# Another order of issue, and other engines for some steps, in a pooled-attention and gated-MLP kernel

## Chip, core and metric

The kernel runs on one core of one Trainium2 chip. The metric is device time in microseconds (us): the median over runs of the whole program. A core has five engines with queues of their own: TensorE (PE, matmuls; PEld are its weight loads), VectorE (DVE), ScalarE (ACT), GpSimd (POOL) and SyncE (SP), which here issues nearly all transfers.

## What is computed

Eight batches of attention with pooled keys and values, then a gated MLP whose gate mixes tokens:

```python
# pool = 8, B, H, S, D = 8, 8, 576, 64
k_p = k.reshape(B, H, S // 8, 8, D).mean(axis=3)
v_p = v.reshape(B, H, S // 8, 8, D).mean(axis=3)
attn = softmax(q @ k_p.T / sqrt(D))              # over the 72 pooled keys
x = (attn @ v_p)                                 # heads side by side: 576 x 512
u, v = split(gelu_tanh(x @ w_in), 2)             # 576 x 512 each
v_n = (v - mean) / sqrt(var + 1e-6) * g_ln
v_s = einsum('ts,bsd->btd', w_sg, v_n) + b_sg[None, :, None]
out = x + (u * v_s) @ w_out
```

All in 32-bit precision; `w_in` and `w_out` arrive as 64-bit floats and are cut into a high and a low 32-bit part on the chip. Every large product is the sum of three matmuls (high by high, high by low, low by high).

## The kernel before, in words

One core does the eight batches one after the other. The work of a batch is cut into steps, each a generator that issues some instructions and then yields. A hand-kept list, `ORDER`, names at each place which step goes on by one piece: `S1+3` is the next piece of step S for pair of heads 1 in batch 3. The lower-case names are the preparation of weights, once for the kernel. As every engine takes its queue in order, `ORDER` sets what each engine does after what. The last lines of the kernel tie each instruction to the one before it on its engine.

The steps of a batch, in the order of the data:

- A, B, C, E load keys, values, one pair's queries (a tile qT, four of them in turn) and the left-over values (through `load`, L234, on SyncE's queue). K sums the keys by eight (`sum8`, L355 on VectorE as one reduction, L358 and L359 on GpSimd as three additions) and lays them out for two heads (kbd); P does the same for values. In batch 0 both are matmuls.
- S (four, one for each pair of heads): scores (TensorE, into PSUM), the maximum (L486, VectorE), the softmax and a copy of a part (el, L503, GpSimd). T and L turn the result over, from batch 1 on through VectorE's 32x32 transpose and HBM. V multiplies by the values, and copies and splits the result into a high and a low part (xhl), with a small tile xta beside it.
- J (batch 0) and H (five blocks of tokens): the v half of the first projection, gelu, mean and variance, scaling, and the split into vhh and vhl. U (four): the u half. W (four): the token mixing into PSUM; then L695 and L697 on VectorE gate it with u, and ghi and glo are split from that. O (four): the second projection, and the sum with x. Z stores.
- Weights: v0 to v3 and u0 to u3 prepare w_in, o0 to o3 w_out, s0 to s4 w_sg. A piece of v, u or o is: one scaling on ScalarE (L275), three integer operations on VectorE (L277, L278, L279), a rounding on ScalarE (L283), then three operations called low, topd and lo below (L222 or L224, L231, L231). lv0, lv1, lu0, lu1, lo0, lo1 load a megabyte each, ls0 and ls1 the w_sg.

The second list, `OTHER`, is a set of keys. A helper that finds its key in it puts its operation on the other of two engines:

| helper | key in `OTHER` | key not in it |
|---|---|---|
| copy (L209, L211) | VectorE | ScalarE |
| move (L215, L217) | GpSimd | ScalarE |
| lower and lowest (low) | VectorE, one operation (L222) | ScalarE (L228) and GpSimd (L224) |
| combine (L231: topd, lo, the low parts) | VectorE | GpSimd |
| sum8 | VectorE, one reduction | GpSimd, three additions |
| normal (L443) | GpSimd | VectorE |
| soften, expo, total | VectorE adds and sums (L448, L462), one exponential (L453) | ten exponentials on ScalarE (L457) |
| scaled | VectorE (L467) | a short one on VectorE (L470), ScalarE (L471) |

A digit for the batch in a key is capped: m3x, k3x, V3x and the like stand for batches 3 to 7, G2x, W2x, H2x and g2x for batches 2 to 7. Exponential and gelu need different tables on ScalarE: where the two follow each other in its queue, `ready` (L204) puts a table load between them.

TensorE's order in batch 0 is: keys and scores, pooled values, T, L and V, then J, H4, U0 to U3 and W0 to W3, with the scores of batch 1 in between. From then on the S, T, L, V of the next batches run between H, U, W and O of the one before.

Of the kernel before, what the change touches and what calls it, by code (L numbers as in the profile page):

```python
# [37 lines left out]
W3+0 W3+0 V0+1 W2+0 A0+3 S2+2 L0+1 K0+3 W3+0 T1+1 T3+1 V0+1 S0+2 S0+2 O0+0 V0+1 T1+1 V0+1 T1+1 S2+2 S2+2 O0+0 V1+1
V1+1 T2+1 O0+0 O1+0 T2+1 S3+2 T0+2 T2+1 O1+0 V2+1 S2+2 P1+2 S1+2 E0+2 O2+0 T3+1 O2+0 O1+0 S3+2 S1+2 S1+2 T3+1 T3+1
V2+1 O3+0 O3+0 Z1+0 O2+0 K0+3 V1+1 O3+0 V3+1 V3+1 V3+1 V2+1 H0+1 H1+1 T0+2 S3+2 S2+2 H0+1 T0+2 V2+1 S3+2 C0+3 T1+2  # L40
V3+1 A1+3 C2+3 S0+3 S3+2 H0+1 L0+2 V1+1 H1+1 H1+1 P2+2 B0+3 H2+1 P2+2 P2+2 H0+1 L0+2 H2+1 H0+1 T0+2 S0+3 P2+2 H3+1
H4+1 H0+1 H3+1 L0+2 H1+1 H1+1 P2+2 H1+1 K1+3 L0+2 K1+3 S1+3 U0+1 Z0+0 V0+2 H3+1 H4+1 H4+1 U1+1 U0+1 C1+4 H2+1 B1+3
H3+1 H4+1 H2+1 T3+2 U1+1 L0+2 T1+2 Z3+0 Z2+0 U2+1 H3+1 U3+1 P0+3 H4+1 H4+1 T2+2 S1+3 T1+2 T1+2 V1+2 H2+1 U2+1 P1+3
U3+1 H2+1 A0+4 H3+1 V0+2 H4+1 H4+1 A1+4 W0+1 T2+2 S0+3 K1+4 W1+1 W0+1 T2+2 K0+4 V0+2 T2+2 E0+3 V1+2 V2+2 W1+1 W0+1
S2+3 V2+2 V1+2 V2+2 S2+3 C3+3 S0+3 T3+2 T3+2 T3+2 W2+1 K0+4 V3+2 S0+3 S1+3 T0+3 T0+3 S3+3 S1+3 V3+2 W3+1 W2+1 V3+2
H0+2 W3+1 V3+2 W1+1 W3+1 W2+1 V0+2 S2+3 S2+3 W0+1 W1+1 W3+1 S1+3 W2+1 P2+3 P2+3 P2+3 H0+2 H1+2 H1+2 H2+2 H0+2 C0+4
H2+2 C2+4 V2+2 T0+3 B0+4 S3+3 S0+4 H1+2 T1+3 T2+3 S0+4 S2+3 S3+3 P2+3 O0+1 O0+1 S3+3 S3+3 O1+1 H0+2 O0+1 Z0+1 O1+1
O1+1 P2+3 T0+3 H1+2 O2+1 H0+2 O2+1 V1+2 S1+4 L0+3 H2+2 L0+3 H1+2 H0+2 O2+1 H1+2 H3+2 S0+4 H3+2 H4+2 S0+4 S0+4 S1+4
H3+2 O3+1 O3+1 H4+2 L0+3 L0+3 H4+2 V0+3 H4+2 L0+3 H4+2 H4+2 P0+4 O3+1 U0+2 U1+2 T1+3 C1+5 Z1+1 Z2+1 T1+3 U0+2 U1+2
T0+4 T1+3 V1+3 T2+3 U2+2 U2+2 U3+2 Z3+1 T2+3 V1+3 H3+2 H3+2 H2+2 T2+3 B1+4 C3+4 H2+2 H2+2 V0+3 V0+3 V1+3 V1+3 K1+4  # L50
H4+2 H3+2 T3+3 H4+2 W0+2 S2+4 U3+2 W0+2 V2+3 S2+4 S1+4 W1+2 S2+4 S2+4 V2+3 A0+5 S3+4 S3+4 E0+4 S3+4 W1+2 W2+2 W2+2
K0+5 W2+2 W3+2 P1+4 T3+3 T3+3 T3+3 V3+3 W3+2 W0+2 W0+2 V2+3 W2+2 V3+3 T0+4 W3+2 W3+2 V3+3 H0+3 W1+2 A1+5 W1+2 S1+4
S1+4 H0+3 H0+3 T1+4 S3+4 S3+4 B0+5 C0+5 H1+3 H1+3 C2+5 O0+2 O0+2 O0+2 Z0+2 H0+3 V0+3 H0+3 H0+3 S2+4 T2+4 O1+2 O1+2
O1+2 V3+3 L0+4 L0+4 O2+2 O2+2 O2+2 O3+2 O3+2 V2+3 H1+3 P2+4 P2+4 P2+4 Z2+2 T0+4 K0+5 H1+3 H1+3 H1+3 O3+2 L0+4 Z1+2
S0+5 S0+5 H2+3 H2+3 T0+4 H3+3 K1+5 L0+4 L0+4 S1+5 H4+3 H3+3 P2+4 P2+4 C3+5 H3+3 H4+3 V0+4 H4+3 H3+3 E0+5 S0+5 P2+5
Z3+2 H4+3 U0+3 U0+3 H4+3 U1+3 S1+5 U1+3 C1+6 U2+3 H4+3 U3+3 S0+5 H4+3 T1+4 T1+4 U2+3 K1+5 V0+4 H2+3 H2+3 T1+4 V1+4
V1+4 U3+3 H4+3 H2+3 P0+5 H3+3 S0+5 T2+4 T3+4 C3+6 T2+4 H3+3 T2+4 A0+6 H2+3 W0+3 S2+5 S1+5 W0+3 W0+3 W0+3 V2+4 W1+3
W2+3 S2+5 V2+4 V2+4 S1+5 W1+3 T3+4 T3+4 T3+4 V3+4 B1+5 P1+5 A1+6 W1+3 V0+4 W1+3 W2+3 T0+5 C0+6 T0+5 P2+5 T1+5 W3+3
V1+4 W3+3 V3+4 V3+4 W3+3 V0+4 P2+5 S3+5 K0+6 S2+5 H0+4 H0+4 S2+5 H1+4 H2+4 S3+5 B0+6 H0+4 H1+4 W2+3 W2+3 V1+4 O0+3
W3+3 T2+5 H2+4 S3+5 O0+3 K0+6 H1+4 H1+4 H0+4 O0+3 S3+5 H2+4 H0+4 H2+4 T0+5 O1+3 O1+3 O2+3 O1+3 V3+4 Z1+3 P0+6 S0+6  # L60
O2+3 Z0+3 T0+5 S1+5 O3+3 V2+4 H0+4 O3+3 S0+6 P2+5 C2+6 S2+5 H1+4 O2+3 Z2+3 H1+4 O3+3 S3+5 P2+5 L0+5 H2+4 L0+5 S1+6
H3+4 H4+4 H3+4 K1+6 H4+4 H4+4 S1+6 U0+4 U0+4 U1+4 H4+4 H4+4 L0+5 L0+5 V0+5 U1+4 L0+5 U2+4 U3+4 S0+6 T1+5 T3+5 U2+4
C1+7 Z3+3 B1+6 H3+4 H3+4 T1+5 T1+5 V1+5 H4+4 H4+4 H3+4 H4+4 H3+4 T2+5 H2+4 W0+4 W0+4 S0+6 U3+4 W1+4 V0+5 K1+6 V1+5
T2+5 T2+5 P1+6 W1+4 A0+7 W1+4 W1+4 S1+6 E0+6 P2+6 S0+6 K0+7 V2+5 V2+5 V2+5 S2+6 S2+6 W2+4 W3+4 V2+5 T3+5 B0+7 W2+4
T3+5 T3+5 V3+5 V3+5 V1+5 W3+4 W3+4 V0+5 A1+7 S3+6 V3+5 K0+7 V1+5 W2+4 H0+5 H1+5 S2+6 W0+4 V3+5 S1+6 W3+4 T0+6 H0+5
W0+4 W2+4 S3+6 O0+4 H1+5 K1+7 S3+6 P2+6 K1+7 O0+4 P2+6 C0+7 T1+6 O1+4 O0+4 S0+7 C2+7 O1+4 T0+6 H1+5 H0+5 B1+7 O1+4
Z1+4 H0+5 S3+6 S3+6 S2+6 Z0+4 H1+5 H1+5 H2+5 H3+5 H2+5 T2+6 V0+5 O2+4 O2+4 S2+6 O2+4 Z2+4 H0+5 H0+5 H1+5 H3+5 S1+7
# [768 lines left out]
```

## Time and profile before

| | |
|---|---|
| median of 3 runs | 581.48 us (579.4 to 582.49) |
| the profiled execution | 582.18 us |
| its span, first to last instruction | 580.5 us |
| TensorE busy, mean granted clock | 538.5 us, 0.977 |
| VectorE, ScalarE, GpSimd busy | 429.4, 270.2, 280.3 us |

The span is 1.7 us short of the time of the same execution. The page gives the share of each engine, then the same in 40 slices of 14.5 us; the view by windows gives it for stretches of one's own choice, with the clock that TensorE was granted (1.00 is the higher of its two levels). A matmul counts as busy from start to modelled end, so TensorE's busy share says where it waits, not how fast it could be.

### The profile page before, as it was taken

The numbers are of one execution on the slowest core, as the hardware profiler recorded it, in microseconds if no ns is written. First come the engines' busy times: TensorE is split into PE (matmuls) and PEld (weight loads), VectorE is DVE, ScalarE is ACT, GpSimd is POOL, SyncE is SP. The second block draws the span as 40 slices with busy tenths as digits, with TensorE's granted clock in tenths as the row PEclk, the third lists the DMA queues.
The fourth block names the chain that finished last, engine by engine and source line by source line (L and its number), as shares of the span: only waits on it lengthen the run. The fifth ranks groups of instructions, "written<-read, shape, count | busy, mean of one in ns | idle before, by whom it ended". The sixth has DMA issues, their size and how long they took to land.

```text
span 580.5 us, 9490 instructions
## 1 busy us (share of the span) xinstructions
PE 538.5 (93%) x3552; PEld 502.9 (87%) x3552; DVE 429.4 (74%) x639; ACT 270.2 (47%) x533; POOL 280.3 (48%) x350
## 2 busy tenths in 40 slices
...
DVE  1799999898877898477978977678796876454252
...
GB/s 289 350 255 177 98 64 29 132 132 116 159 168 164 118 66 118 162 51 133 166 74 160 159 71 73 190 98 130 135 87 42 62 93 93 42 21 42 0 1 103
DMA packets 43134, 67.08 MB, mean 116 GB/s; under 512 B 5776, under 2 KB 22160, under 8 KB 43088
## 3 DMA queue, kind: packets, MB, share of 16 engines
...
q8 instruction: 28, 0.46, 0.3%
...
q14 instruction: 18, 0.15, 0.1%
...
## 4 chain that ended last, share of the span: by engine, by line
PE 59%; DVE 26%; DMA 4%; POOL 4%; issue 3%; ACT 2%; SPq 1%; DVEq 0%; POOLq 0%; ACTq 0%
PE mps L133 50%; PE aps L133 9%; DVE nmax L486 2%; DVE top L278 2%; DVE e L448 1%; SPq L234 1%; DVE ssum L462 1%; DVE bst L644 1%; DVE xhl L231 1%; DVE raw L279 1%; DVE al L561 1%; DVE top L231 1%; DMA al<-tfar 1%; DVE y L509 1%; DMA kraw<-in_k 1%
## 5 line engine op out<-in xcount | busy, mean ns | idle before, releaser
L133 PE MATMUL mps<-xhl,wih 128*128 128x288 f32 x512 | 90.2, 298 | 6.2 <-ACT vg L640 4.9
L133 PE MATMUL mps<-wih,xhl 128*128 128x512 f32 x256 | 84.4, 400 | 3.7 <-DVE xhl L231 2.4
L133 PEld LDWEIGHTS mps<-xhl,wih 128*128 128x128 f32 x512 | 75.9, 190 | 7.7 <-ACT vg L640 5.4
L443 POOL TENSOR_TENSOR e<-e,ssum 128x720 f32<-128x720 f32 x24 | 35.9, 1499 | 61.6 <-DVE ssum L442 61.6
L133 PEld LDWEIGHTS mps<-wih,xhl 128*128 128x128 f32 x256 | 47.7, 188 | 16.1 <-DVE xhl L231 3.9
L133 PE MATMUL mps<-wsh,vhh 128*128 128x288 f32 x256 | 56.5, 303 | 1.6 <-ACT u L681 1.6
L133 PE MATMUL mps<-wsh,vhl 128*128 128x288 f32 x256 | 55.9, 300 | 1.7 <-DVE vhl L231 1.7
L133 PE MATMUL mps<-wsl,vhh 128*128 128x288 f32 x256 | 56.0, 301 | 0.0
L133 PE MATMUL mps<-xhl,wil 128*128 128x288 f32 x256 | 54.8, 295 | 0.0
L133 PE MATMUL mps<-ghi,woh 128*128 128x288 f32 x240 | 51.6, 295 | 2.0 <-DVE x L733 2.0
L647 POOL TENSOR_TENSOR rstd<-mv,eps 128x1 f32<-128x1 f32 (+1 forms) x40 | 10.2, 255 | 86.1 <-DVE mv L645 84.4
L133 PE MATMUL mps<-glo,woh 128*128 128x288 f32 x240 | 51.4, 295 | 0.3 <-POOL glo L231 0.2
L133 PE MATMUL mps<-ghi,wol 128*128 128x288 f32 x240 | 51.3, 295 | 0.0
L133 PE MATMUL mps<-wil,xhl 128*128 128x512 f32 x128 | 50.5, 395 | 0.0
L231 POOL TENSOR_TENSOR xhl<-x,xhl 128x576 fp32r<-128x576 f32 x23 | 32.9, 1435 | 34.2 <-ACT x L211 30.6
L695 DVE SCALAR_TENSOR_TENSOR mps<-mps,gcol,bbc 128x576 f32<-128x576 f32 x32 | 26.3, 821 | 29.9 <-PE mps L133 29.7
L231 POOL TENSOR_TENSOR glo<-u,ghi 128x576 fp32r<-128x576 f32 x17 | 25.4, 1506 | 42.2 <-ACT ghi L211 38.3
L133 PE MATMUL aps<-kbd,qT 128*128 128x144 f32 x300 | 43.4, 293 | 1.9 <-ACT x L211 1.7
L133 PEld LDWEIGHTS mps<-wsh,vhh 128*128 128x128 f32 x256 | 42.4, 195 | 1.9 <-ACT u L681 1.8
L133 PEld LDWEIGHTS mps<-wsh,vhl 128*128 128x128 f32 x256 | 42.3, 194 | 2.0 <-DVE vhl L231 2.0
L133 PEld LDWEIGHTS aps<-kbd,qT 128*128 128x128 f32 x300 | 40.3, 194 | 3.6 <-ACT x L211 2.4
L644 DVE BATCH_NORM_STATS2 bst<-vg 128x6 f32<-128x512 f32 (+1 forms) x40 | 27.2, 680 | 20.9 <-ACT vg L637 11.6
...
## 6 DMA issues: line engine op xcount, KB each, us to landing
...
```

The costliest lines, as they stand in the source:

```text
L133: nc.tensor.matmul(o, lhsT, rhs, start=start, stop=stop)
L231: (nc.vector if key in OTHER else nc.gpsimd).tensor_tensor(o, x, y, op=op)
L234: queue.dma_start(o, i)
L278: nc.vector.scalar_tensor_tensor(top, high, -0x80000000, top, op0=ALU.bitwise_and, op1=ALU.bitwise_or)
L279: nc.vector.tensor_scalar(high, top, -0x800000, None, op0=ALU.bitwise_and)
L443: (nc.gpsimd if key in OTHER else nc.vector).tensor_tensor(e, e, rec.unsqueeze(3).broadcast_to([P, NT, 2, SP]), op=ALU.mult)
L448: nc.vector.tensor_tensor(e, every.rearrange("p s (h k) -> p s h k", h=2), nmax.unsqueeze(3).broadcast_to([P, NT, 2, SP]), op=ALU.add)
L462: nc.vector.tensor_reduce(out=ssum, in_=e, axis=AX.X, op=ALU.add)
L486: nc.vector.tensor_reduce(out=nmax, in_=every.rearrange("p s (h k) -> p s h k", h=2), axis=AX.X, op=ALU.max, negate=True)
L644: nc.vector.bn_stats(bst, vg)
L647: nc.gpsimd.tensor_tensor(rstd, mv[:, 1:2], eps[:n, 1:2], op=ALU.add)
L695: nc.vector.scalar_tensor_tensor(vs, vs, gcol[:, d:d + 1], bbc.rearrange("p (a n) -> p a n", a=2), op0=ALU.mult, op1=ALU.add)
```

## The change

Both lists are replaced. `ORDER` has the same 1252 entries, each as often as before, in another order. `OTHER` had 104 keys and has 117: 57 come in and 44 go out. No helper and no step is altered. The start of `ORDER` and the whole of `OTHER`:

```diff
 ORDER = """
-A0+0 C0+0 E0+0 lv0 v1 v1 A1+0 K0+0 K0+0 S0+0 H0+0 H1+0 v1 C1+0 S1+0 B0+0 S0+0 K1+0 v1 S0+0 B1+0 A0+1 C2+0 S1+0 S1+0
-S0+0 v0 C3+0 lv1 K0+1 v0 S1+0 K1+0 K0+1 S0+0 S1+0 T0+0 A1+1 S2+0 S2+0 v0 v3 v0 T0+0 P0+0 ls0 S2+0 S2+0 L0+0 s2 s3
-P1+0 s0 P0+0 lu0 B0+1 C0+1 L0+0 lo0 P1+0 V0+0 v3 v2 T1+0 E0+1 v2 s1 V0+0 V0+0 K1+1 S2+0 v3 s0 s1 v2 S3+0 S3+0 J0+0
-v2 s3 T1+0 V1+0 s2 v3 S3+0 u0 P0+1 u1 S3+0 u1 T2+0 V1+0 T2+0 u1 V1+0 S3+0 L1+0 T3+0 L1+0 u1 B1+1 V2+0 T3+0 u0 lu1 u3
-P1+1 u3 V2+0 u0 C1+1 u0 A0+2 V0+0 V3+0 S0+1 S0+1 u3 V3+0 u2 K0+2 C3+1 V2+0 u2 K1+1 u3 S0+1 S0+1 V2+0 J1+0 J2+0 V3+0
-J3+0 o1 o1 u2 u2 H1+0 H2+0 H1+0 C2+1 S1+1 S2+1 H0+0 H0+0 A1+2 K1+2 o1 P2+1 V1+0 P2+1 V3+0 H3+0 S1+1 H3+0 o0 H1+0 o0
-H1+0 o0 ls1 S0+1 H1+0 H2+0 S1+1 C0+2 o1 H4+0 U0+0 S3+1 H0+0 H0+0 H2+0 H0+0 H4+0 S2+1 o0 lo1 S2+1 H4+0 H3+0 U1+0 C1+2
-U0+0 C3+2 B0+2 o3 K0+2 H4+0 S1+1 U1+0 U2+0 B1+2 U3+0 S2+1 S1+1 o2 o3 S2+1 H2+0 H2+0 H4+0 o2 o2 s4 o3 H3+0 o2 P2+1
-T0+1 H2+0 H3+0 H3+0 H4+0 S3+1 C2+2 T0+1 H4+0 o3 H4+0 S0+2 U2+0 U3+0 T1+1 S3+1 s4 S0+2 W0+0 S3+1 S3+1 W0+0 L0+1 P2+1
...
+lv0 A0+0 v0 v0 E0+0 A1+0 C0+0 v1 v1 v1 v1 v0 K0+0 lv1 B0+0 K0+0 A0+1 v3 v0 v2 S0+0 S0+0 K1+0 v3 v2 C1+0 S0+0 K1+0 v3
+S0+0 C2+0 B1+0 K0+1 S1+0 S1+0 lu0 S2+0 S2+0 v2 K0+1 S1+0 S1+0 S0+0 S2+0 T0+0 v2 P0+0 v3 P0+0 S1+0 L0+0 S2+0 T0+0
+L0+0 P1+0 P1+0 V0+0 A1+1 ls0 s1 u0 u1 K1+1 s0 B0+1 C3+0 C1+1 lo0 V0+0 T1+0 T1+0 u0 u0 u1 s2 S3+0 S3+0 K1+1 S3+0 C2+1
+V0+0 V1+0 s2 B1+1 V1+0 lu1 J0+0 s1 ls1 u0 s0 C3+1 S2+0 u1 S3+0 S3+0 u2 T2+0 T2+0 P0+1 L1+0 L1+0 T3+0 V2+0 C0+1 T3+0
+u2 u2 s3 V1+0 u1 V2+0 u2 u3 A0+2 o0 H0+0 H1+0 H2+0 u3 V2+0 s4 o0 J1+0 u3 V3+0 V3+0 J2+0 V3+0 J3+0 u3 o0 s4 H0+0 H0+0
+V1+0 S0+1 o0 P1+1 H1+0 V3+0 S1+1 V2+0 E0+1 H2+0 o1 A1+2 V0+0 S0+1 S0+1 H0+0 H0+0 S1+1 H3+0 H1+0 H4+0 S2+1 S1+1 S0+1
+H0+0 H2+0 H3+0 S2+1 H1+0 o1 S3+1 lo1 H1+0 H1+0 o1 o1 o2 H4+0 H4+0 s3 C0+2 P2+1 P2+1 U0+0 U0+0 H4+0 K0+2 S2+1 H4+0
+H3+0 o3 U1+0 U2+0 U1+0 U2+0 P2+1 o2 H3+0 S0+1 o2 H3+0 H2+0 H4+0 H2+0 o3 o2 U3+0 U3+0 S2+1 T0+1 H2+0 S3+1 S2+1 C1+2
+T0+1 H4+0 o3 H3+0 S3+1 o3 H4+0 S1+1 S1+1 W0+0 W0+0 K1+2 K1+2 S3+1 W0+0 S3+1 B0+2 C3+2 T1+1 P0+2 L0+1 W1+0 P2+1 C2+2
...
 """.split()

 OTHER = set("""
-G00 G01 G12 G13 H00 H01 H03 H13 H21 H23 V00 V01 V11 V13 V33 W02 W03 W10 W20 W21 X10 X11 X20 X21 X30 X31 X32 c10 c12
-c22 g00 g04 g10 g13 g14 g21 g22 g23 g24 h11 h20 k10 k31 l2 l3 m00 m02 m10 m12 m21 m22 m23 m30 m31 m32 m33 n00 n01
-n11 n12 n13 n20 n21 n22 n23 n30 n31 n32 o0d o1m o2a o2d o2m o3a s0d s2 s2d s3 u0a u0d u0m u1a u1d u1m v0d v2a v2d
-v2m v3a x11 x13 x20 x21 x23 z00 z04 z11 z14 z22 z23 z31 z32 z33 z34
+G10 G12 G20 G21 G23 H00 H01 H03 H10 H11 H20 H23 V00 V02 V03 V12 V13 V21 V23 V30 V33 W01 W02 W11 W12 W13 W20 W21 W22
+W23 X10 X11 X12 X13 X20 X22 X23 X30 X31 X32 X33 c11 c22 g11 g14 g20 g22 g23 g24 h20 h21 k10 k11 k20 k21 l1 l2 l3 m01
+m11 m21 m22 m23 m30 m31 m32 m33 n00 n02 n10 n11 n20 n21 n22 n23 n30 n31 n32 o1d o1m o2d o2m p10 p11 s0d s1 s1d s2d
+s4d u0m u1a u1d u1m u2a u2d u2m u3d u3m v0a v0d v0m v1a v1d v1m v2a v2m v3a z00 z03 z11 z12 z14 z20 z24 z30 z32 z34
 """.split())
```

Told by the table above, the keys do this before the first gating of batch 0 (`W0+0`): on VectorE come in two key sums, two value sums and a left-over sum, four low, one topd, two splits of w_sg and one of xhl; from it go two soften and two total, two copies to vhh and one to w_sg. Ten-fold exponentials are then issued for six S steps instead of four. Counted through the list, the exponential and the gelu change places 35 times on ScalarE instead of 29.

## Rows read from the trace of the kernel before

**Rows 1.** The page, parts 1 and 2: busy time, share and count; tenths in 40 slices.

```profile
PE 538.5 (93%) x3552; PEld 502.9 (87%) x3552; DVE 429.4 (74%) x639; ACT 270.2 (47%) x533; POOL 280.3 (48%) x350
...
DVE  1799999898877898477978977678796876454252
```

**Rows 2.** The view by windows: stretch, length, each engine's busy time, clock, DMA share, GB/s.

```profile
0.00:14.50 14.50, 7.42 (x31) 7.29 (x32) 1.76 (x4) 3.89 (x7) 7.78 (x28) 1.00 0.86 290
14.50:106.78 92.28, 69.74 (x373) 58.06 (x372) 87.60 (x120) 62.42 (x170) 65.28 (x65) 0.91 0.49 163
107.00:215.00 108.00, 103.18 (x676) 96.43 (x676) 91.33 (x138) 49.25 (x101) 62.05 (x75) 0.97 0.46 130
215.00:560.00 345.00, 342.61 (x2364) 325.85 (x2363) 242.55 (x371) 153.07 (x254) 142.32 (x181) 1.00 0.32 94
```

**Rows 3.** Timeline of VectorE (start, length, group): first score maximum, first gating of batch 0.

```profile
14.57 0.91 DVE L486 TENSOR_REDUCE nmax<-mps 128x10 f32<-128x720 f32 x1 [1.87 <-PE mps L133]
...
106.78 0.80 DVE L695 SCALAR_TENSOR_TENSOR mps<-mps,gcol,bbc 128x576 f32<-128x576 f32 x1
```

**Rows 4.** Groups by form, VectorE, 14.5 to 106.8: busy, mean ns | idle before.

```profile
L278 DVE SCALAR_TENSOR_TENSOR top<-raw,top 128x512 int32<-128x512 int32 x11 | 11.8, 1077 | 0.4
L279 DVE TENSOR_SCALAR raw<-top 128x512 int32<-128x512 int32 x11 | 9.7, 882 | 0.4
...
L222 DVE SCALAR_TENSOR_TENSOR raw<-raw 128x512 f32<-128x512 uint32 x5 | 5.2, 1044 | 0.0
L231 DVE TENSOR_TENSOR top<-top,wih 128x512 f32<-128x512 f32 x4 | 5.2, 1300 | 0.0
L231 DVE TENSOR_TENSOR wil<-raw,top 128x512 fp32r<-128x512 f32 x4 | 4.2, 1043 | 0.1
L462 DVE TENSOR_REDUCE ssum<-e 128x10 f32<-128x720 f32 x4 | 3.5, 887 | 0.3 <-ACT e L453 0.3
L231 DVE TENSOR_TENSOR top<-top,woh 128x512 f32<-128x512 f32 x2 | 3.4, 1684 | 0.0
...
L231 DVE TENSOR_TENSOR wol<-raw,top 128x512 fp32r<-128x512 f32 x2 | 2.5, 1248 | 0.0
...
L355 DVE TENSOR_REDUCE kp<-kraw 128x144 f32<-128x1152 f32 x1 | 1.3, 1294 | 0.0
```

**Rows 5.** Weight tiles `top` and `raw`, VectorE: ns min/median/max, first and last start.

```profile
L278 DVE SCALAR_TENSOR_TENSOR top<-raw,top x12: 691/693/1787, 11.6 to 91.9; 128x512 int32<-128x512 int32 x12
...
L231 DVE TENSOR_TENSOR top<-top,wih x4: 679/1314/1892, 26.0 to 57.7; 128x512 f32<-128x512 f32 x4
...
L279 DVE TENSOR_SCALAR raw<-top x12: 427/428/1940, 12.3 to 92.7; 128x512 int32<-128x512 int32 x12
...
L222 DVE SCALAR_TENSOR_TENSOR raw<-raw x5: 686/949/1466, 40.2 to 94.6; 128x512 f32<-128x512 uint32 x5
```

**Rows 6.** Groups by form, GpSimd, the same stretch as in rows 4.

```profile
L224 POOL TENSOR_TENSOR raw<-raw 128x512 f32<-128x512 f32 x6 | 6.8, 1125 | 3.0 <-DVE raw L279 1.6 <-issue 1.1 <-ACT raw L228 0.2
...
L443 POOL TENSOR_TENSOR e<-e,ssum 128x720 f32<-128x720 f32 x4 | 5.9, 1488 | 5.2 <-DVE ssum L442 5.2
```

**Rows 7.** Timelines of TensorE, SyncE's queue and ScalarE: first matmul, weight load, weight step.

```profile
6.29 1.86 PE L133 MATMUL mps<-pool,kraw 128*128 128x16 f32 x8 [6.29 <-DMA kraw<-in_k]
...
1.83 0.57 SPq L234 DMA_DIRECT2D raw<-in_moe_w_in  x1
...
10.40 0.66 ACT L275 ACTIVATE top<-raw 128x512 f32<-128x512 f32 x1 [7.66 <-DMA raw<-in_moe_w_in]
```

**Rows 8.** ScalarE: table loads (groups); timeline: one wide exponential, first and last of ten.

```profile
L204 ACT ACT_TABLE_LOAD x29 | 37.2, 1283 | 0.5
...
16.46 0.80 ACT L453 ACTIVATE e<-e 128x720 f32<-128x720 f32 x1 [3.56 <-DVE e L448]
...
40.29 0.32 ACT L457 ACTIVATE e<-aps,nmax 128x72 f32<-128x72 f32 x1 [4.01 <-DVE nmax L486]
...
42.96 0.37 ACT L457 ACTIVATE e<-aps,nmax 128x72 f32<-128x72 f32 x1
```

More of the change, by code (lines that the diff above doesn't have):

```diff
@@ L38 @@
[L38 to L67, printed above, removed]
@@ new lines @@
+K0+3 O1+0 V0+1 O0+0 O2+0 E0+2 S3+2 T3+1 A1+3 S0+2 K1+3 O2+0 S2+2 T2+1 V2+1 C0+3 S1+2 T3+1 O3+0 T0+2 Z1+0 S2+2 S1+2
+V2+1 K0+3 S3+2 S3+2 V2+1 O2+0 V0+1 C1+3 O3+0 T3+1 T3+1 S0+3 V3+1 V3+1 O3+0 P2+2 S2+2 V3+1 H0+1 H1+1 T0+2 H0+1 S2+2
+S3+2 T1+2 S3+2 V3+1 H0+1 H2+1 B1+3 V1+1 Z2+0 H1+1 H1+1 H0+1 B0+3 V2+1 L0+2 S0+3 T2+2 H2+1 P2+2 H1+1 H1+1 H3+1 H1+1
+H0+1 H0+1 Z3+0 T0+2 P2+2 Z0+0 P2+2 P2+2 T0+2 L0+2 H3+1 H3+1 H4+1 H4+1 H4+1 H4+1 H4+1 E0+3 L0+2 S1+3 C2+3 H3+1 H3+1
+H2+1 L0+2 H2+1 U0+1 U1+1 L0+2 U0+1 H2+1 H2+1 V0+2 C0+4 U2+1 U1+1 U3+1 T1+2 S0+3 T1+2 P0+3 S1+3 T1+2 U2+1 H4+1 H4+1
```

55 lines of the change are left out of this document (40 added, 15 removed).

## Prediction, made before the changed kernel was run

> **What bounds the kernel now.** I read the page's shares first, then the slices, then the view by windows, and only then single instructions. TensorE is busy for 93% of the span [rows 1], but that is a mean over two stages. From 215 to 560 us it is busy for 342.6 of 345 us at a clock of 1.00 [rows 2]: all that could be won there is 2.4 us. From 14.5 to 106.8 us, from the first score maximum to the first gating of batch 0 [rows 3], it is busy for only 69.7 of 92.3 us at a mean clock of 0.91, and there VectorE is busy for 87.6 us, with 4.7 us idle [rows 2]. Before that, up to 14.5 us, VectorE did 1.8 us of work [rows 2]; the slices show the same as 1, then 7 and then nines [rows 1]. So the start is bound by VectorE, the rest by TensorE, and a change of order and engines must win in the start or not at all.
>
> What is VectorE's time made of in that stretch? The view by form gives a mean for each kind of weight operation [rows 4], the view by tile its least duration [rows 5]. The integer operation L278 takes 0.69 us alone and up to 1.79; its mean is 1.08. L279 takes 0.43 to 1.94, with a mean of 0.88. The largest excesses, 1.1 and 1.5 us, are as long as one two-input operation of GpSimd, 1.1 to 1.5 us [rows 6], and GpSimd is busy for 65.3 of the 92.3 us [rows 2]; so I read them as VectorE held up by one GpSimd operation. The excess over the least, by mean less least times count, is: L278 11 x 0.386 = 4.2, L279 11 x 0.455 = 5.0, L222 5 x 0.358 = 1.8, L231 of the same size 4 x 0.62 + 4 x 0.36 + 2 x 1.0 + 2 x 0.57 = 7.1 us. That is 18.1 us [rows 4, 5]. Other kinds have some excess too; I leave it in their means. So VectorE's own work is 87.6 - 18.1 = 69.5 us, and 18 us is time in which it is held up by GpSimd.
>
> **The change, part by part: up to the first gating.** I count the entries of both lists up to W0's second piece. TensorE has the same matmuls ahead of it, but for one score step and their order, so it does not decide.
>
> (a) Work that moves to VectorE there: five sums at no more than 1.29 us each (L355, 6.5), four low at 0.69 (2.8), one topd at 0.68, and three subtractions of 576 columns, at 0.68 x 576/512 = 0.76 (2.3): 12.3 us [rows 4, 5]. Work that leaves: two soften, two total and one maximum over the same 720 scores, at 0.89 (4.5), and six smaller ones (two copies to vhh, one to w_sg, a transposition, two on ten columns), at half of that each as an estimate (2.7): 7.2 us [rows 4]. Net 5.1 us more.
>
> (b) Work that moves into VectorE's early hole. The changed list puts the whole of v0 and v1 ahead of the first maximum, where before there were three operations of v1. A whole one is 0.43 + 0.69 + 0.43 + 0.69 + 0.68 + 0.68 = 3.6 us (L277 taken as L279), so 7.2 in place of 1.55: 5.6 us leave the stretch [rows 5]. The hole is 12.7 us long [rows 2], so it hides them, if the weight is there.
>
> (c) For that the weight load goes out first, and the keys after it. Before, TensorE started at 6.29 us, when the keys landed; the weight, issued at 1.83, let ScalarE start at 10.40 [rows 7]. A megabyte at the 290 GB/s of that window [rows 2] is 3.6 us. So the keys, the scores and the first maximum come between 1 us (the load overlaps their latency) and 3.6 us later; I take 2.5, since the same queue carries both. The maximum is then at 14.57 + 2.5 = 17.1 us.
>
> (d) GpSimd is relieved: ahead of the first gating it has 23 operations that read two tiles in place of 50. At 1.1 us (L224) to 1.5 us (L443) [rows 6] the 27 are 30 to 40 us of its 65. VectorE's own exposed operations stay about as many (68 after the early ones, against 67). If the excess goes by GpSimd's count it falls to 46%, if by its time to between 38 and 54%; I take half, 9.0 us. The bounds are 3 (they hardly meet) and 18 (they meet as often).
>
> (e) VectorE's idle time in the stretch was 4.7 us [rows 2]; the row of the first maximum shows what such a wait is, 1.9 us for TensorE [rows 3]. I take 5, with bounds of 3 and 12.
>
> Sum: 69.5 + 5.1 - 5.6 + 9.0 + 5 = 83.0 us, from 17.1 to 100.1. Before it ended at 106.8: 6.7 us are won.
>
> **The rest.** After the first gating TensorE has the same work left, at full clock, so the 6.7 us should reach the end. In each later batch VectorE gets some 2 us more (subtractions and copies that come over, less one key sum and two scalings that leave). I cost this at nothing: from 215 to 560 us VectorE idles for 102 us, some 19 in each batch [rows 2]. If that cover were gone, the 2 us would show in each of six batches. The keys for GpSimd's small copies and the places of loads and stores in SyncE's queue change too; transfers take a third of the share there [rows 2], and I cost them at nothing, with 2 us either way as bounds.
>
> ScalarE gets six more table loads, 35 for 29. A load is 1.28 us in each of its 29 rows, and the engine stood idle for 0.5 us in all ahead of them [rows 8], so six are 7.7 us on an engine that is under half busy [rows 1]. The Trainium skill (ScalarE: Activation LUTs, What ACT_TABLE_LOAD costs) puts a drain of 1.38 us beside the load and the whole switch at some 2.7 us, and its section on table sets asks that calls be batched by set, which speaks against this change. By it the six would be an estimated 16 us; the sum above would be the same, as both lie beside other work. This trace shows no such drain ahead of the loads.
>
> The profiled execution took 582.2 us, 0.7 above the median. 582.2 - 6.7 = 575.5 against it; against the median of 581.5, 574.8.
>
> **Rivals.**
>
> *More than that is won.* If GpSimd and VectorE hardly meet, the excess is 3 and the idle 3: 75.0 us, to 92.1, 14.7 us won. Another 2 to 3 could come from 107 to 215 us, where TensorE still waits for 4.8 us [rows 2], as GpSimd's load falls in batches 1 and 2 too. That gives 581.5 - 17 = 564.5. For it speaks that so much leaves GpSimd; against it, that VectorE carries more.
>
> *The gain is eaten on VectorE.* It is in order, and its queue now holds reductions over keys and values that must wait for loads, with weight work behind them. If its idle time is 11 us rather than 5, or the excess stays at 15, the first gating is at 106: 581. This is also the case that the moved work is only worth what it costs.
>
> *Slower: ScalarE becomes the bound of the start.* In the stretch it is busy for 62.4 us and idle for 29.9 [rows 2]. Two more tenfold exponentials, from 40.29 to 43.33 or 3.0 us each against one of 0.80, are 4.5 us, and two of the six new loads fall here, 2.6 [rows 8]; the other moves about cancel. That makes 69.5 us. The tens and loads stand between the gelu, the scaling and the copy to vhh of batch 0, for which TensorE waits at the first W. It decides once ScalarE's idle time is above 106.8 - 17.1 - 69.5 = 20 us of the 30 it had. With 26 the gating is at 112.6: 5.8 us later, or 587. It is the result that the Trainium skill's rule on table sets would point to.
>
> **How the numbers follow.** The forecast (571 to 578.5, point 574.8) has a chance of 0.45; more won, 0.18; eaten, 579 to 584, 0.24; ScalarE, above 584, 0.13. Half a percent, 2.9 us, is about what a measurement of this kernel can tell from no change, so faster is below 578.6 and slower above 584.4. Faster has 0.62 (nearly all of the first, and the second), same 0.25, slower 0.13. The range of 563 to 586 leaves out the far end of the second case and most of the last one's, some 0.15.
>
> **What would show it.** L486's first row at about 17 us and the first L695 near 100; L278 and L279 with means near 0.85 and 0.65 rather than 1.08 and 0.88; GpSimd under half busy in between; TensorE's first matmul at 8 to 9 us; 35 table loads, with no long idle of TensorE behind them; and from 215 us on TensorE waiting no more than now. I am wrong if the first gating comes earlier and the end does not, if the excess stays though GpSimd has less to do, or if the idle rows of TensorE around 60 to 100 us name ScalarE.

## The result, and the profile after

The changed kernel takes 557.49 us (median of 4 runs, 556.64 to 558.14) against 580.44 us (4 runs, 579.06 to 582.49): the ratio is 0.960, with a 95% interval of 0.957 to 0.964. That is 23 us faster; 6.7 us were forecast, and the time lies below the range. The spans of the two profiled executions are 580.5 and 556.4 us, 24.1 us apart. The page after (parts 1 and 2), to be set beside [rows 1]:

```profile
PE 531.2 (95%) x3552; PEld 500.6 (90%) x3552; DVE 420.4 (76%) x674; ACT 278.8 (50%) x569; POOL 239.6 (43%) x323
...
DVE  5688999778879779787777987885878956574262
```

VectorE now works from the first slice on, and the unbroken run of nines in the start is gone. The timeline of the changed kernel (start, length, group) gives the marks of the sum, beside [rows 3, 7]: the weight load's issue, the weight's first use, the first matmul, the first maximum; the view of line L695 (least, median and greatest ns, first and last start) the first gating.

```profile
0.81 0.44 SPq L234 DMA_DIRECT2D raw<-in_moe_w_in  x1
...
6.15 0.68 ACT L275 ACTIVATE top<-raw 128x512 f32<-128x512 f32 x1 [4.07 <-DMA raw<-in_moe_w_in]
...
8.56 1.86 PE L133 MATMUL mps<-pool,kraw 128*128 128x16 f32 x8 [8.56 <-DMA kraw<-in_k]
...
16.85 0.91 DVE L486 TENSOR_REDUCE nmax<-mps 128x10 f32<-128x720 f32 x1 [2.67 <-PE mps L133]
```

```profile
L695 DVE SCALAR_TENSOR_TENSOR mps<-mps,gcol,bbc x32: 766/822/828, 90.3 to 539.1; 128x576 f32<-128x576 f32 x32
```

The first gating is at 90.28 instead of 106.78 us: 16.5 us. The other 7.6 us are won behind it. The view by windows (stretch, length, busy time of each engine, clock, DMA share, GB/s) shows both, first before from the first gating on, then after:

```profile
106.78:580.50 473.72, 461.29 (x3152) 437.55 (x3151) 340.04 (x517) 203.89 (x357) 207.27 (x258) 0.99 0.34 101
```

```profile
16.85:90.28 73.43, 65.80 (x369) 56.50 (x370) 66.02 (x112) 63.68 (x194) 35.05 (x38) 0.98 0.50 165
...
90.28:556.40 466.12, 457.94 (x3154) 436.76 (x3153) 347.11 (x550) 209.60 (x366) 198.37 (x260) 0.99 0.36 107
215.00:540.00 325.00, 324.92 (x2250) 310.59 (x2249) 239.81 (x381) 135.80 (x220) 124.38 (x166) 1.00 0.31 90
```

Behind the first gating TensorE has the same work, 3152 and 3154 matmuls. It idles for 473.72 - 461.29 = 12.4 us before and 8.2 after, in both with some 5.2 us at the very end, and the matmuls themselves take 3.4 us less. The granted clock gives an estimated 2 us of that: before, two stretches of 4 us behind the gating ran near its lower level, after, one. In the same columns, first before, then after:

```profile
106.78:110.78 4.00, 4.00 (x19) 4.00 (x19) 3.18 (x6) 3.95 (x24) 3.50 (x5) 0.53 0.41 95
174.78:178.78 4.00, 3.92 (x18) 3.88 (x18) 3.01 (x6) 1.39 (x3) 0.47 (x1) 0.57 0.94 300
```

```profile
90.28:94.28 4.00, 4.00 (x32) 4.00 (x32) 3.90 (x7) 2.88 (x15) 2.81 (x3) 1.00 0.79 276
112.28:116.28 4.00, 3.69 (x15) 3.46 (x16) 3.08 (x6) 3.09 (x6) 1.56 (x2) 0.60 0.11 19
```

The first of these stretches belongs to the start: before, TensorE was busy for only 1.85 of the 4 us ahead of the first gating and ran at 0.53 for the 4 us behind it; in the changed kernel it was busy throughout and stays at 1.00. In the stretch up to the gating, 92.2 us have become 73.4. VectorE's groups by form there (busy us, mean ns | idle before), beside [rows 4]:

```profile
L278 DVE SCALAR_TENSOR_TENSOR top<-raw,top 128x512 int32<-128x512 int32 x10 | 6.9, 693 | 0.3
...
L222 DVE SCALAR_TENSOR_TENSOR raw<-raw 128x512 f32<-128x512 uint32 x7 | 4.8, 687 | 0.0
L277 DVE TENSOR_SCALAR top<-top 128x512 int32<-128x512 int32 x10 | 4.8, 476 | 1.1 <-ACT top L275 1.1
L279 DVE TENSOR_SCALAR raw<-top 128x512 int32<-128x512 int32 x10 | 4.3, 428 | 0.3
...
L231 DVE TENSOR_TENSOR wil<-raw,top 128x512 fp32r<-128x512 f32 x4 | 2.7, 691 | 0.2
L467 DVE SCALAR_TENSOR_TENSOR vg<-vg,mv,rstd 128x512 f32<-128x512 f32 x2 | 2.6, 1280 | 0.4 <-POOL rstd L648 0.4
```

The weight operations now have the least durations of [rows 5] as their means, but for L277 (0.48, 0.42 alone): the collisions are not halved but nearly gone. Four rows still meet something, one of L277, one of L467 (1.81 us beside another of 0.75) and two of L441 (1.2 us each beside others of 0.17). In what follows VectorE's *excess* in a run is, over its groups from the first maximum to the first gating, the mean less the time alone, times the count, with 0.69 us alone for L278, 0.425 for L277 and L279, 0.685 for L222, 0.68 for the 512-column and 0.75 for the 576-column L231 (0.665 for vhl), 0.75 for L467 (0.73 with 64 rows), 0.47 for L428, 0.68 for L663, 0.40 to 0.43 for the copies of L209, 0.17 for the one- to ten-column L441 and L470; the other groups keep their means in all these runs. By it before has 24.7 us and after 3.9. (Durations of neighbours overlap a little, so busy less excess is good to about 1 us.)

### The profile page after: what moved, and what is told of

It is laid out like the page before. It is cut to its first block, busy times and chain, and to the rows that moved or that the text cites. A ratio compares the mean times of both kernels' runs of the same rounds, so it can differ in the third digit from the quotient of the medians.

```text
span 556.4 us, 9530 instructions
## 1 busy us (share of the span) xinstructions
PE 531.2 (95%) x3552; PEld 500.6 (90%) x3552; DVE 420.4 (76%) x674; ACT 278.8 (50%) x569; POOL 239.6 (43%) x323
## 4 chain that ended last, share of the span: by engine, by line
PE 82%; ACT 6%; DVE 5%; DMA 4%; issue 1%; SPq 1%; POOL 1%; DVEq 0%; ACTq 0%
PE mps L133 68%; PE aps L133 13%; DMA qT<-in_q 1%; DMA al<-tfar 1%; DMA kraw<-in_k 1%; ACT e L457 1%; ACT L204 1%; SPq L234 1%; DVE al L561 1%; PE aps L176 1%; DVE wsl L231 0%; ACT vg L640 0%; DVE y L509 0%; ACT top L275 0%; ACT kbd L377 0%
## 5 line engine op out<-in xcount | busy, mean ns | idle before, releaser
L133 PEld LDWEIGHTS mps<-wih,xhl 128*128 128x128 f32 x256 | 48.0, 188 | 11.6 <-DVE xhl L231 0.6
L133 PE MATMUL mps<-wsh,vhh 128*128 128x288 f32 x256 | 54.8, 295 | 0.0
L133 PE MATMUL mps<-wsl,vhh 128*128 128x288 f32 x256 | 54.7, 294 | 0.0
L133 PE MATMUL mps<-wsh,vhl 128*128 128x288 f32 x256 | 54.5, 294 | 0.0
L647 POOL TENSOR_TENSOR rstd<-mv,eps 128x1 f32<-128x1 f32 (+1 forms) x40 | 13.1, 328 | 76.5 <-DVE mv L645 67.3
L695 DVE SCALAR_TENSOR_TENSOR mps<-mps,gcol,bbc 128x576 f32<-128x576 f32 x32 | 26.1, 816 | 23.1 <-PE mps L133 23.1
L640 ACT ACTIVATE vg<-mps 128x512 f32<-128x512 f32 x32 | 19.1, 596 | 48.1 <-PE mps L133 43.5
L133 PEld LDWEIGHTS mps<-xhl,wil 128*128 128x128 f32 x256 | 41.0, 188 | 0.0
L133 PEld LDWEIGHTS mps<-wsh,vhl 128*128 128x128 f32 x256 | 40.9, 188 | 0.0
L133 PEld LDWEIGHTS mps<-wsh,vhh 128*128 128x128 f32 x256 | 40.9, 188 | 0.0
```

The costliest lines, as they stand in the source:

```text
L133: nc.tensor.matmul(o, lhsT, rhs, start=start, stop=stop)
L640: nc.scalar.activation(vg, o, AF.Gelu_apprx_tanh)
L647: nc.gpsimd.tensor_tensor(rstd, mv[:, 1:2], eps[:n, 1:2], op=ALU.add)
L695: nc.vector.scalar_tensor_tensor(vs, vs, gcol[:, d:d + 1], bbc.rearrange("p (a n) -> p a n", a=2), op0=ALU.mult, op1=ALU.add)
```

## The experiments

The kernel before, measured beside each group of runs, had medians of 581.1 to 581.7 us. In microseconds, from each profiled execution (busy, excess and idle are VectorE's, and GpSimd's busy time, between first maximum and first gating):

| run | time | first max | gating | busy | excess | idle | GpSimd |
|---|---|---|---|---|---|---|---|
| before | 581 | 14.6 | 106.8 | 87.6 | 24.7 | 4.6 | 65.2 |
| changed | 557.5 | 16.9 | 90.3 | 66.0 | 3.9 | 7.4 | 35.1 |
| order_new_keys_old | 616.7 | 16.7 | 114.3 | 71.7 | 12.0 | 25.9 | 52.8 |
| order_old_keys_new | 614.4 | 14.6 | 109.7 | 83.0 | 11.7 | 12.1 | 38.0 |
| after_gpsimd_reads | 571.3 | 17.2 | 104.7 | 81.3 | 19.5 | 6.2 | 63.6 |
| after_gpsimd_writes | 562.7 | 16.4 | 96.8 | 71.9 | 9.8 | 8.5 | 61.0 |
| after_sums_back | 562.8 | 16.6 | 96.3 | 68.2 | 11.3 | 11.6 | 48.7 |
| before_sums_as_fills | 575.8 | 15.0 | 102.3 | 81.3 | 18.1 | 6.0 | 59.7 |
| before_sums_on_vector | 580.0 | 14.8 | 106.4 | 85.8 | 16.3 | 5.7 | 47.1 |
| after_v_behind_max | 564.9 | 16.9 | 96.5 | 71.2 | 3.9 | 8.4 | 35.0 |

**Order and keys apart, start and rest apart.** The first two runs put one list of the change on the other of the kernel before; the next two join the lists at the first gating.

```diff
 # order_new_keys_old                # order_old_keys_new
-ORDER: before                       -OTHER: before
+ORDER: changed                      +OTHER: changed
 # start_new_rest_old: changed up to W0+0's second piece, then what is left in the order of before;
 #   keys of weights and batches 0 and 1 changed, of batches 2 on as before
 # start_old_rest_new: the other way round
```

> The changed order with the old engine keys. Theory K (the gain comes from fewer two-input operations of GpSimd, whatever their places): GpSimd does as much as before, so the first gating stays near 105 us and the time near 578. Theory O (the gain comes from the places: early weight work, and GpSimd's operations put where VectorE does not meet them): first gating near 93, time near 562. Theory P (order and keys were fitted to each other, and either alone is worth little): VectorE waits for results that GpSimd now makes late, and the time is 580 or above.

> The old order with the new engine keys. Theory K: L278 and L279 go down to means near 0.75 and 0.5 us, the first gating comes near 94 us, time near 564. Theory O: the moved work makes VectorE's queue longer in the start, the excess stays above 12 us, time 578 or above. Theory P: as for O, 580 or above.

> The changed order up to the first gating of batch 0 with the new keys of the weights and of batches 0 and 1; after it the old order, with the old keys of the later batches. If the start is worth 17 us and the rest 7, as the two traces read: 564. If the 7 us of the rest come only from being ahead of VectorE's backlog after the start: 558. If the new start is paid back in the old rest: above 570.

> The old order and keys up to the first gating, the new ones after it. If the start is worth 17 us and the rest 7: 574. If the rest owes its 7 us to the start: 581.

Either half alone is slower by some 6%: 616.67 us, ratio 1.061 (1.059 to 1.062), and 614.44, 1.058 (1.056 to 1.059). With the new start and the old rest the first gating is at 92.99, so the start's gain is there, and the time is 579.72 (ratio 0.998, 0.996 to 0.999): 485.7 us are left behind the gating, where the changed kernel has 466.1 and the kernel before 473.7. With the old start and the new rest it is 588.34, slower than before (1.012, 1.009 to 1.015), where 574 or 581 were expected. So neither the two lists nor the two stretches add up: in these four runs an order won only with the keys it came with, and a rest only behind the start it came with. Which waits make up the losses behind the gating was not taken apart.

```profile
16.74:114.30 97.56, 71.01 (x359) 60.68 (x359) 71.68 (x112) 61.62 (x167) 52.84 (x57) 0.86 0.41 135
```

```profile
14.61:109.67 95.06, 72.65 (x376) 62.65 (x376) 82.98 (x127) 66.91 (x209) 38.02 (x40) 0.84 0.50 161
```

Those are the windows of the first two runs up to the first gating (columns as above). New order with old keys: VectorE is little busier than in the changed kernel, 71.7 us, but idles for 25.9; 9.9 of it are three waits for GpSimd's longer queue (rstd 4.2, top 3.6 and 2.1 us). Old order with new keys: VectorE has 83.0 us to do, as v0 and v1 are not done early. The order alone takes the excess from 24.7 to 12.0 us, a factor of 0.49; the keys alone to 11.7, 0.47; both to 3.9, 0.16, where 0.49 x 0.47 is 0.23. So fewer reads and other places each take about half, and both together take more than either. How much of the order's half is the places is not shown: the long idle time of the first run lets VectorE and GpSimd meet less too, and 41 of GpSimd's operations with two inputs lie in its stretch, against 48 before.

**Reads and fills on GpSimd.** The changed kernel with 27 more operations on GpSimd in the start, once as additions that read two inputs, once as fills of the same length.

```diff
+            if 21 <= k < 210 and (k - 21) % 7 == 0:
+                nc.gpsimd.tensor_tensor(dmy, ones, ones, op=ALU.add)     # after_gpsimd_reads
+                nc.gpsimd.memset(dmy, 0.0); nc.gpsimd.memset(dmy, 0.0)   # after_gpsimd_writes
```

> The changed kernel with 27 more additions on GpSimd, of two 128x512 inputs each, into a tile that nobody reads, one behind every seventh entry of the order from S0+0's maximum on; so GpSimd again has 50 operations that read two tiles ahead of batch 0's first gating, as before the change, where the changed kernel has 23. Theory C (collisions follow the number of GpSimd's two-input operations): the means of L278 and L279, 0.69 and 0.43 us in the changed kernel, go back towards 1.08 and 0.88, VectorE's busy time in the stretch from 66 towards 80 us, the first gating from 90.3 to some 100 to 105, and the time to 567 to 573 us. Theory Q (what counts is who waits for GpSimd's queue, not collisions): the means stay within 0.1 us, and the first gating moves by as much as in the run with writes in the same places. Theory P (the order places GpSimd's reads where VectorE has no two-input work): means rise, but by less than half of the way, and the time by 3 to 8 us.

> The same places as in the run with 27 more additions, each now two fills of a tile that nobody reads: GpSimd is as long busy, but reads nothing. Theory C: the means of L278 and L279 stay at 0.69 and 0.43, and the time within 3 us of the changed kernel's 557.5. Theory Q: the same delay as with the additions, some 5 to 15 us, as the results that VectorE and TensorE wait for come later from GpSimd's queue.

571.25 us (ratio 0.984, 0.981 to 0.986) and 562.72 (0.970, 0.967 to 0.972). The fills cost 5.2 us, more than theory C had (within 3), and reading costs 8.5 us on top. The 5.2 us are not the longer queue by itself: with the fills VectorE is busy for 71.9 us instead of 66.0 and idle for only 1.1 us more, so most of what the stretch grew by is collisions again, some with the fills, some with GpSimd's own reading operations, which now meet VectorE at other places (L222 below, with one row of 1.88 us beside a subtraction). Groups by form in the stretch, reads first (lines stand 3 further down here: L281 is L278):

```profile
L281 DVE SCALAR_TENSOR_TENSOR top<-raw,top 128x512 int32<-128x512 int32 x10 | 9.8, 980 | 0.3
L282 DVE TENSOR_SCALAR raw<-top 128x512 int32<-128x512 int32 x10 | 6.8, 680 | 0.3
...
L776 POOL TENSOR_TENSOR dmy<-ident 128x512 bf16<-128x512 f32 x25 | 28.6, 1143 | 0.9
```

```profile
L281 DVE SCALAR_TENSOR_TENSOR top<-raw,top 128x512 int32<-128x512 int32 x10 | 6.9, 692 | 0.3
L225 DVE SCALAR_TENSOR_TENSOR raw<-raw 128x512 f32<-128x512 uint32 x7 | 6.0, 853 | 0.0
L280 DVE TENSOR_SCALAR top<-top 128x512 int32<-128x512 int32 x10 | 5.7, 573 | 1.1 <-ACT top L278 1.1
...
L282 DVE TENSOR_SCALAR raw<-top 128x512 int32<-128x512 int32 x10 | 5.1, 509 | 0.3
...
L776 POOL MEMSET dmy<- 128x512 bf16 x25 | 13.8, 552 | 0.7
L777 POOL MEMSET dmy<- 128x512 bf16 x25 | 13.4, 537 | 1.4
```

For 28.6 us of additions VectorE is busy 81.27 - 71.93 = 9.3 us longer than for 27.2 us of fills. The operation with two inputs, L278, is held up with the additions and not with the fills (0.98 against 0.69); the ones with a single tile, L277 and L279, are with the fills too (0.57 and 0.51, where the changed kernel has 0.48 and 0.43).

**The six sums, put back and moved alone.** Keys k11, k20, k21, p10, p11 and l1 are 18 of GpSimd's reading operations.

```diff
 # after_sums_back: the changed kernel          # before_sums_on_vector: the kernel before
-OTHER: k11 k20 k21 p10 p11 l1                  +OTHER: k11 k20 k21 p10 p11 l1
 # before_sums_as_fills: the kernel before, in sum8 for these six keys, each of the three additions:
-            nc.gpsimd.tensor_tensor(t[..., 0:n], t[..., 0:n], t[..., n:2 * n], op=ALU.add)
+            nc.gpsimd.memset(t[..., 0:n], 0.0); nc.gpsimd.memset(t[..., 0:n], 0.0)
```

> The changed kernel with six of its keys undone (k11, k20, k21, p10, p11, l1): the sums over eight keys or values of batch 1, and over the keys of batch 2, are again three additions on GpSimd in place of one reduction on VectorE. VectorE has 6.5 us less of its own work, GpSimd some 16 us more, and 18 more operations that read two tiles. Theory C: excess comes back for 18 of the 27 operations, 7 to 10 us, so VectorE gains nothing net; first gating at 91 to 95, time 558 to 563. Theory Q: the sums stand in GpSimd's queue ahead of the low parts and of vhl that batch 0 waits for: VectorE idles for over 10 us more in the stretch, the gating goes past 97, and the time is above 565.

> The kernel before with the same six sums moved to VectorE as the change does, and nothing else of the change. VectorE gets 6.5 us of its own work at no more than 1.29 us each and loses 6 to 8 us of excess: theory C gives a first gating within 2 us of 106.8 and a time within 3 us of 581. Theory P (moved work must have its place in the order; a reduction that waits for its load holds VectorE's queue): slower by over 3 us, as the whole set of keys on the old order is slower by 33 us.

> The kernel before with the 18 additions on GpSimd of six sums over eight (keys and values of batch 1, keys of batch 2) each replaced by two fills of the same place, so that GpSimd is about as long busy but reads nothing for them; this part of the computation (those sums) is left out, and their results are zero. Theory C (VectorE's excess comes from GpSimd's reads): 18 of 50 reading operations less, so some 6 to 8 us of the 18 us of excess go, the means of L278, L279 and L231 fall by 0.1 to 0.3 us, and the first gating comes at 99 to 102 instead of 106.8; of that the time keeps what the rest lets through, 573 to 579. Rival (the excess has another source): means and gating within 1 us of before.

After: 562.75 (0.969, 0.967 to 0.971), gating 6.0 us later. Five of the sums lie in the stretch, 5.8 us by their rows; VectorE gives these up and is yet 2.1 us busier, as 7.4 us of excess come back, and its idle time is 4.1 us longer. Before: the sums alone on VectorE take 8.4 us of excess from it, 24.7 to 16.3, give it 7.0 us of work (three more kp at 1.32, two vp at 1.21, one vlp at 0.67), and win almost nothing: 579.98 (0.998, 0.996 to 0.999), gating 106.4. With the sums as fills GpSimd is busy 5.5 us less than before, VectorE has the same work, and 6.3 us of its busy time go: gating 102.3, 575.83 us (0.989, 0.985 to 0.994). So in the kernel before, too, it was the reading. One reading operation of GpSimd cost VectorE 6.3 / 18 = 0.35 us against fills, 8.4 / 18 = 0.47 against none, and 7.4 / 15 = 0.49 when five sums came back.

**The early hole and the weight load.** Terms (b) and (c) undone in the changed kernel, one at a time, and the load cut in two.

```diff
 # after_v_behind_max
-lv0 A0+0 v0 v0 E0+0 A1+0 C0+0 v1 v1 v1 v1 v0 K0+0 lv1 B0+0 K0+0 A0+1 v3 v0 v2 S0+0 S0+0
+lv0 A0+0 v0 E0+0 A1+0 C0+0 v1 v1 K0+0 lv1 B0+0 K0+0 A0+1 S0+0 S0+0 v0 v1 v1 v0 v0 v3 v2
 # after_keys_first
-lv0 A0+0 v0 v0 E0+0 A1+0
+A0+0 E0+0 lv0 v0 v0 A1+0
 # after_half_load: lv0 loads raw[:, 0:1]; A0+0, behind its own load, loads raw[:, 1:2]
```

> The changed kernel with nine of VectorE's eleven or so early operations of v0 and v1 (the bit operations of v0, and the low, the subtraction and the addition of both) put behind the first maximum, as in the kernel before, where only v1's bit operations stood ahead of it; term (b) alone undone. Theory B (the early hole hides them): 1.55 + 2 x 2.06 = 5.7 us come back into the stretch; the first maximum stays at 16.8, the first gating goes from 90.3 to 95 to 97 and the time to 562 to 564 us. Rival: VectorE's 7.4 us of idle time in the stretch take most of it, gating within 2 us and the time below 560.

> The changed kernel with the first keys and their rest (A0+0, E0+0) ahead of the weight load lv0 in SyncE's queue, as in the kernel before; term (c) alone undone. Theory C1 (the weight load ahead of the keys cost 2.5 us and bought the early work on v0 and v1): TensorE's first matmul goes from 8.6 back to 6.3 us, but the weight comes some 2 us later, and VectorE, whose maximum stands behind the weight operations in its queue, has its first maximum at 17 to 19; the gating and the time within 3 us of 90.3 and 557.5, rather later. Rival: the start is bound by the keys; the maximum comes at 14.6 and the time falls by 2 us.

> The changed kernel with the first weight load cut in two halves of 512 KB and the first keys' load between them: the half that v0 reads, the keys, the half that v1 reads. Theory B: the keys land some 1 to 2 us earlier, TensorE's first matmul is at 7 to 7.6 in place of 8.56 us, the first maximum at 15.3 to 16, VectorE's early work on v0 and v1 still fits, and the first gating is about 1 us earlier than 90.3; the time 556 to 557. Rival: v1's bit operations come later by as much, the maximum stands behind them in VectorE's queue and nothing is won.

The early work behind the maximum: 564.93 us (0.972, 0.969 to 0.975), gating 96.5; 6.2 us come back where 5.7 were expected, 5.2 as VectorE's work and 1.0 as idle time, and the time loses 7.4. The keys first: 560.11 (0.963, 0.960 to 0.966), first maximum not earlier but later, at 20.0, gating 93.2. This run does not undo (c) alone. Its first matmul starts at 5.96 us, 2.6 earlier, but the first queries are loaded from ScalarE's queue, behind the scaling of the weight, which now waits for the later weight (ScalarE's queue, then TensorE, then VectorE):

```profile
10.19 0.38 ACTq L234 DMA_DIRECT2D qT<-in_q  x1
...
17.24 2.74 PE L133 MATMUL mps<-kbd,qT 128*128 128x144 f32 x10 [6.55 <-DMA qT<-in_q]
...
20.02 0.91 DVE L486 TENSOR_REDUCE nmax<-mps 128x10 f32<-128x720 f32 x1 [2.02 <-PE mps L133]
```

In the kernel before this load went out at 0.81, in the changed one at 6.16. VectorE has done v0 and v1 by 18.0 here and waits for the scores. The halves: first maximum 18.3, gating 92.7, 558.21 us (0.961, 0.957 to 0.965), not to be told from the changed kernel. The timeline of the run with the halves says why:

```profile
7.81 1.86 PE L133 MATMUL mps<-pool,kraw 128*128 128x16 f32 x8 [7.81 <-DMA kraw<-in_k]
...
10.43 0.66 ACT L279 ACTIVATE top<-raw 128x512 f32<-128x512 f32 x1 [3.50 <-DMA raw<-in_moe_w_in]
...
11.79 0.59 PE L133 MATMUL mps<-pool,raw 64*128 64x8 f32 x2 [2.11 <-DMA raw<-in_kv]
```

The keys land 0.75 us earlier, but the weight's second half only at 10.43, and the rest of the keys at 11.8, where the changed kernel's matmul on them started at 10.35. The maximum waits for the last of them.

**The keys of the later batches.** In the changed kernel the keys of batches 2 and later are put back: all 30 (the first expectation says 33), then the seven subtractions, then the 20 copies and scalings.

```diff
 # after_late_keys_old: all of the following and k20 k21 k31
 # after_late_subs_old
-OTHER: H20 V21 V23 V30 W22 W23
+OTHER: H21
 # after_late_copies_old
-OTHER: G20 G21 G23 X22 X23 X33 g20 h21 z20 z24 z30
+OTHER: X21 g21 x20 x21 x23 z22 z23 z31 z33
```

> The changed kernel with the keys of batch 2 and later as before the change (33 of them differ), and the order, the weights' keys and those of batches 0 and 1 as changed. The first gating stays within 1 us of 90.3 (nothing ahead of it differs but the sums over batch 2's keys). Theory F (order and keys are fitted to each other everywhere): TensorE waits again in every batch from 215 us on, some 20 to 35 us in all, and the time is 578 to 592 us. Theory S (only the start's keys matter, since VectorE has 20 us of slack in each later batch): within 3 us of 557.5.

> The changed kernel with the seven subtractions of batches 2 and later that changed engines undone (H20, H21, V21, V23, V30, W22, W23: six from VectorE back to GpSimd, one the other way). All 30 keys of these batches undone together took 23 us (that run's expectation says 33; it is 30). Theory L (the length of GpSimd's queue ahead of results that TensorE waits for): these six, at 1.4 to 1.5 us each and batch on GpSimd against 0.75 to 0.95 on VectorE, carry most of it: over 12 us, 570 us or more, and TensorE's waits name GpSimd. Theory F (every key is fitted to its place, no kind in particular): some 5 to 10 us, 563 to 567.

> The changed kernel with the copies and scalings of batches 2 and later that changed engines undone (20 keys: G2x, g2x, h21, x2x, X2x, X33, z2x, z3x), subtractions and sums as changed. Theory L: little, below 5 us, 558 to 562, since they stand on ScalarE and VectorE, which idle for over 50 and 19 us in each of these batches. Theory F: as much as the subtractions, 563 to 570.

All of them: 580.82 us (1.000, 0.998 to 1.001), the whole gain, though the first gating is still at 93.2 (3.0 us later, not within 1: additions for k20 and k21 are back on GpSimd ahead of it). The subtractions: 569.58 (0.980, 0.978 to 0.983); the copies: 568.74 (0.979, 0.977 to 0.981). So 12.1 and 11.2 us, and theory L's "below 5 us" for the copies was wrong: theory F had them alike. Where the subtractions lose, one place shows (GpSimd's timeline, then TensorE's, then the windows around it; idle before and its releaser in brackets):

```profile
254.68 1.96 POOL L358 TENSOR_TENSOR vraw<-vraw 128x512 f32<-128x512 f32 x2 [4.20 <-DMA vraw<-in_v]
256.71 0.42 POOL L359 TENSOR_TENSOR vp<-vraw 128x128 f32<-128x128 f32 x1
...
257.87 1.40 POOL L231 TENSOR_TENSOR glo<-u,ghi 128x576 fp32r<-128x576 f32 x1
```

```profile
259.32 0.85 PE L133 MATMUL mps<-glo,woh 128*128 128x288 f32 x2 [5.97 <-POOL glo L231]
```

```profile
253.30:259.30 6.00, 0.05 (x1) 0.00 (x0) 0.00 (x0) 0.73 (x2) 4.35 (x6) 0.72 0.28 111
259.30:263.00 3.70, 3.68 (x16) 3.68 (x17) 2.76 (x5) 0.00 (x0) 0.33 (x2) 0.53 0.08 18
263.00:267.00 4.00, 4.00 (x33) 4.00 (x33) 1.61 (x4) 0.00 (x0) 3.13 (x6) 1.00 0.46 131
```

The subtraction for glo stands in GpSimd's queue behind a value sum that waits 4.20 us for its load, and TensorE, which takes its own queue in order, waits 5.97 us for glo. Behind that wait its clock is at 0.53 for 3.7 us, near the lower of its two levels (1.2 of 2.4 GHz), then at 1.00 again: 16 matmuls in the 3.7 us, against 33 in the 4.0 that follow. In the changed kernel these subtractions are VectorE's from batch 2 on, and none of TensorE's waits names glo. Where the copies lose, no such place shows: behind the gating TensorE's waits, the longest 1.4 us, name VectorE and ScalarE, none GpSimd.

## Why the prediction was wrong

The direction, the place and the mechanism were right: the start was bound by VectorE, by its collisions with GpSimd, and 16.5 of 24.1 us were won there. Three steps failed: the base of VectorE's own work, the excess after, and the rest at nothing.

*VectorE's own work (the 69.5 us).* Excess was taken out of four kinds of operation, 18.1 us, and that of "other kinds" left in their means. By the full count it was 24.7, so the own work was 87.6 - 24.7 = 62.9. With (a) and (b) as the prediction had them, 62.9 + 5.1 - 5.6 = 62.4; the changed kernel shows 66.0 - 3.9 = 62.1. So (a) and (b) were right within 1 us in sum, (b) also alone (5.6 forecast, 5.2 of work and 6.2 in all lost when undone), and the 6.6 us of excess left in the means made the base too large.

*(d), the excess after.* 9.0 us were taken, half of 18.1; it is 3.9. The count's factor was fair (0.46 by count; the keys alone gave 0.47). What the step left out is the order, which also decides which of GpSimd's reads meet VectorE's operations: the new order alone, with the old keys, left 0.49, not all of it by the places. The lower bound of 3 was the right end, for a reason that the prediction did not price.

*(e), idle.* 7.4 us instead of 5, within its bounds. Together: 62.1 + 3.9 + 7.4 = 73.4 instead of 83.0, and the gating at 90.3 instead of 100.1.

*(c), the load.* The first maximum was forecast at 17.1 and came at 16.85, 2.3 us later than before, and TensorE's first matmul 2.3 us later too. The run with the keys first does not price it: there the maximum waits for scores whose queries stand in ScalarE's queue behind the weight, a dependence that (c) did not name.

*The rest at nothing.* 7.6 us were won there. The prediction had the work behind the gating "at full clock", but its own [rows 2] give a clock of 0.97 and 4.8 us of idle TensorE from 107 to 215 us; it priced these only in a rival, at 2 to 3. TensorE's idle time went from 4.8 to 2.9 us in the first 108 us behind the gating and from 2.4 to 0.1 after that, without the end; the clock gives an estimated 0.47 x 4.00 + 0.43 x 3.92 - 0.40 x 3.69 = 2.1 us (one less the clock, times the busy time, in the windows of 4 us above). That is 6.3 us, some 1.9 of them the clock behind the start's last wait. VectorE's idle time, which was named as the cover, did cover the added work (347.1 us instead of 340.0, with TensorE waiting less), but it is not what sets the time: undoing 30 keys there costs all 23 us, while VectorE still idles for a quarter of the time. TensorE waits for single results, and in the one place taken apart what made the result late was an instruction ahead of it in its queue that waited for a load. The prediction counted what moved between engines and did not ask, per result that TensorE waits for, what is queued ahead of it.

*The rivals.* "More than that is won" put the gating at 92.1 and the time at 564.5; it came true and was exceeded, by 1.8 us at the gating and by 5 in the rest. "The gain is eaten on VectorE" did not: it needed an idle time of 11 us or an excess of 15, and they are 7.4 and 3.9. "ScalarE becomes the bound" did not either: it is busy for 63.7 of 73.4 us and idle for 9.7, where it would have decided from 20 on. The 35 table loads take 1.283 us each, and ScalarE stands idle for 0.6 us in all ahead of them:

```profile
L204 ACT ACT_TABLE_LOAD x35 | 44.9, 1283 | 0.6
```

The drain of 1.38 us that the Trainium skill (ScalarE: Activation LUTs, What ACT_TABLE_LOAD costs) puts beside each load does not show in this trace either.

*What stays open.* 1.3 of the 7.6 us behind the gating are not found, and how much of them belongs to which key or place was not taken apart beyond the two kinds; the losses of the runs with half a change overlap, so they are no shares of the gain.
